# A gated linear recurrence and a two-layer block on one core: the last four groups of the block with seven products for eight, 64-column state products, and another written order

## The chip, the cores and the metric

The kernel runs on one core of one Trainium2 chip. A core has a matrix engine (PE), a vector engine (DVE), a scalar engine (ACT), GpSimd (POOL) and a queue for transfers (SP). The metric is the device time of one execution in microseconds (us), as the median of several runs. Each engine takes its instructions strictly in the order in which they were written for it; engines wait for each other through semaphores. SBUF is the working memory of 128 partitions; PSUM has eight banks of 2 KB in each partition, and only PE writes products there.

## The reference

```python
B, H, S, D = 4, 8, 768, 48          # batch, heads, tokens, head size
mag = sqrt(a_re**2 + a_im**2); scale = minimum(mag, 0.999) / (mag + 1e-6)
a = (a_re + 1j * a_im) * scale
for t in range(S):                   # for every batch and head
    S_re, S_im = a[t][:, None] * state  (+ outer(k[t], v[t]) on the real part)
    y[t] = q[t] @ S_re               # 48 values
x = y as (B * S, H * D) = (3072, 384)
h = x @ w_in                         # (384, 2048)
g = maximum(h, 0) + alpha * minimum(h, 0)
out = g @ w_out                      # (2048, 384), float32 throughout
```

## The kernel before

**Two halves in one stream.** The recurrence is cut into 24 units (4 batches of 6 chunks of 128 tokens, all 8 heads at once). A unit (`unit`, line 645) rotates keys and queries on DVE, meets them in six levels by small products (`meet`, L680, into the two PSUM banks of tag "lv"), transposes the keys (L789, bank "misc"), copies them to `T` on ACT (L791), forms the state's update from `T` and `V` (L799, `ps_kv`, banks "misc" and "lv"), and sums the unit's result in `ps_y` (two banks of tag "y"; L819 and L843). The result goes through `T` to a buffer in DRAM (`ysc`, L862). Ahead of the units, nine tasks `gates` work out the decays and phases on DVE, ACT and POOL and write them to DRAM (`decs`, `phs`); units read them back.

**The two-layer block.** `all_mlp` (L928) runs over groups of tokens, `sizes` (L642): two groups of one chunk, ten of two chunks, two of one chunk. For each of 16 slices f of 128 hidden values, `features` (L883) adds three products into one PSUM bank of tag "h" (L891; 128 by 128 weights against 256 tokens), ACT takes the negative part (L898) and DVE finishes `g` (L900) in `g_sb`, a ring of 36 places of 128 columns. `outputs` (L905) then adds 16 products of 384 columns for each chunk (L910, bank "o"), ACT copies the sum out (L920) and SP sends it (L923). `features` and `outputs` are called in turn, so that their products alternate on PE. The eight banks are lv 2, misc 1, y 2, h 2, o 1.

**What sets the order.** Every task (nine `gates`, loads, weights, 24 units, x loads, the block) is a generator that yields once for each step, and the string `ORDER` (L30) names the task whose next step is issued; each engine's program is the steps that fall to it, in that order. Letters A to I are the gates, P to Z and a to m the units, n the loads of x, o the block. The arguments of a yield (an engine, a planned duration, events, rings) are a planner's; in this file they do nothing. Where a tile's buffer is in use, the instruction that writes it next waits.

In the written order the last step of the last unit stands 131 letters before the end; 277,248 columns of the block's products stand ahead of it on PE and 17,664 behind it. (A column is one column of the moving operand of one product; a product of f32 shows as two MATMUL records, so L910 has 768 records for 384 products.)

## Time and profile before

| | |
|---|---|
| median of 3 runs | 837.81 us (835.79 to 839.57) |
| the profiled execution | 837.42 us; span from its first to its last instruction 835.7 us |
| mean granted clock of PE | 0.992 |
| busy PE / PEld / DVE / ACT / POOL | 701.3 / 533.9 / 637.5 / 432.4 / 282.6 us |
| busy DVE in L900, the block's only DVE work | 97.9 us |
| last record of a unit on PE | ends at about 796 us |

The page gives the busy time of each engine, the span in 40 slices of 20.9 us with busy shares in tenths, and the costliest groups of instructions, each with the mean duration of one and the idle time that came before them on their engine. A list of instructions in order of time gives start, duration, engine, line, operation and how many were merged. A table by stretches gives busy time and instructions of each engine in each stretch. PEld is the loading of weights, which runs beside PE.

### The profile page before, as it was taken

How to read it: one execution, taken by the hardware profiler on the slowest of the kernel's cores; microseconds unless marked ns; L12 is line 12 of the kernel's file. 1: busy time of each engine (PE TensorE's matmuls, PEld its weight loads, DVE VectorE, ACT ScalarE, POOL GpSimd, SP SyncE). 2: the span in 40 equal slices, each digit the busy share in tenths (PEclk: the TensorE clock that was granted, in tenths of full speed). 3: DMA queues.
4: the chain of work that ended last, by engine and by line, in shares of the span. 5: the costliest groups of instructions: out<-in, count | busy, mean ns of one | idle time of the engine just before them, and what ended most of it. 6: DMA issues, size and time to landing. Idle time of an engine off the chain costs nothing.

```text
span 835.7 us, 25314 instructions
## 1 busy us (share of the span) xinstructions
PE 701.3 (84%) x10784; PEld 533.9 (64%) x10784; DVE 637.5 (76%) x905; ACT 432.4 (52%) x893; POOL 282.6 (34%) x352
## 2 busy tenths in 40 slices
PE   0001317589999999999999999999999999999998
PEld 0001316467777777777777777776777777777776
DVE  5988979999999998989978989896649555542112
ACT  7787678377556644863675366624333333323221
POOL 5379399357306620661453127303220000000000
PEclk9999999699999999999999999999999999999999
DMA  7584975885688479538863966457446635401110
GB/s 221 169 239 133 307 226 135 234 222 147 176 234 199 114 217 250 140 84 245 227 158 83 275 176 162 145 158 186 100 98 176 159 95 125 103 24 36 42 29 10
DMA packets 186984, 130.82 MB, mean 157 GB/s; under 512 B 74744, under 2 KB 177272, under 8 KB 186488
## 3 DMA queue, kind: packets, MB, share of 16 engines
q1 hardware_dynamic: 186872, 129.20, 57.6%
q8 instruction: 85, 1.39, 0.7%
q14 instruction: 27, 0.22, 0.1%
HBM read 100.82 MB, written 35.71 MB: 163 GB/s over the span
## 4 chain that ended last, share of the span: by engine, by line
PE 63%; DVE 12%; POOL 7%; DMA 7%; ACT 6%; issue 3%; SPq 2%; DVEq 0%; ACTq 0%; POOLq 0%
PE ps_o L910 25%; PE ps_h L891 24%; PE ps_lv L680 4%; POOL gate L341 3%; PE ps_kv L799 3%; PE ps_y L819 3%; DMA T<-decs 2%; DVE KQ L718 2%; PE ps_y L843 2%; POOL run L343 2%; DVE gate L341 2%; DMA PP<-phs 1%; DMA phs<-gate 1%; DVE gate L429 1%; PE ps_kt L789 1%
## 5 line engine op out<-in xcount | busy, mean ns | idle before, releaser
L891 PE MATMUL ps_h<-xT,w_in_sb 128*128 128x256 f32 (+1 forms) x1344 | 297.4, 355 | 13.7 <-DMA xT<-ysc 13.5
L910 PE MATMUL ps_o<-w_out_sb,g_sb 128*128 128x384 f32 x768 | 295.0, 499 | 3.3 <-DVE g_sb L900 2.7
L891 PEld LDWEIGHTS ps_h<-xT,w_in_sb 128*128 128x128 f32 x1344 | 234.8, 193 | 85.5 <-DMA xT<-ysc 12.9
L898 ACT ACTIVATE g_sb<-ps_h 128x256 f32<-128x256 f32 (+1 forms) x224 | 79.0, 353 | 214.4 <-PE ps_h L891 213.3
L900 DVE SCALAR_TENSOR_TENSOR g_sb<-g_sb,al,ps_h 128x256 f32<-128x256 f32 (+1 forms) x224 | 97.9, 437 | 118.9 <-ACT g_sb L898 118.3
L910 PEld LDWEIGHTS ps_o<-w_out_sb,g_sb 128*128 128x128 f32 x768 | 136.0, 191 | 56.2 <-DVE g_sb L900 4.6
L718 DVE TENSOR_TENSOR KQ<-KQ,T 96x1024 f32<-96x1024 f32 x120 | 147.8, 1232 | 27.0 <-PE ps_lv L680 16.4
L341 POOL TENSOR_TENSOR gate<-gate 128x72 f32<-128x72 f32 (+1 forms) x56 | 42.5, 759 | 177.2 <-ACT gate L371 170.9
L680 PE MATMUL ps_lv<-WQ 96*32 96x32 f32 x2304 | 34.5, 202 | 76.4 <-DVE WQ L663 53.7
L680 PEld LDWEIGHTS ps_lv<-WQ 96*32 96x32 f32 x2304 | 26.2, 115 | 98.1 <-DVE WQ L663 53.7
L741 ACT COPY WQ<-KQ 96x1024 f32<-96x1024 f32 x48 | 50.0, 1041 | 23.7 <-DVE KQ L718 23.6
L341 DVE TENSOR_TENSOR gate<-gate 128x576 f32<-128x576 f32 (+3 forms) x70 | 46.8, 669 | 1.0
L341 POOL TENSOR_TENSOR gate<-run,runs 128x12 f32<-128x12 f32 x46 | 36.8, 800 | 31.2 <-ACT runs L371 28.1
L757 ACT COPY W<-KQ 96x512 f32<-96x512 f32 x48 | 30.8, 642 | 27.3 <-DVE KQ L718 23.2
L429 DVE TENSOR_TENSOR gate<-gate 128x1152 f32<-128x1152 f32 (+2 forms) x36 | 44.5, 1257 | 0.1
L518 POOL TENSOR_SCALAR top<-top 128x768 f32<-128x768 f32 x16 | 39.7, 2486 | 14.3 <-ACT top L510 14.2
L694 ACT ACTIVATE A<-ps_lv,columns 128x64 f32<-128x64 f32 x144 | 37.6, 335 | 8.4 <-PE ps_lv L680 8.3
L799 PEld LDWEIGHTS ps_kv<-V,T 64*96 64x96 f32 x704 | 35.9, 167 | 9.1 <-issue 4.6
L857 ACT COPY T<-ps_y 48x256 f32<-48x256 f32 x96 | 32.0, 365 | 18.2 <-PE ps_y L843 17.4
L321 POOL TENSOR_TENSOR gate<-gate 128x72 f32<-128x72 f32 (+5 forms) x24 | 22.5, 939 | 54.8 <-DVE gate L321 53.8
L799 PE MATMUL ps_kv<-V,T 64*96 64x48 f32 x704 | 38.9, 252 | 2.1 <-ACT T L791 2.0
L819 PE MATMUL ps_y<-A,VL 64*48 64x64 f32 x2304 | 38.8, 221 | 0.3 <-issue 0.3
(104 smaller groups left out, 943.7 us busy)
## 6 DMA issues: line engine op xcount, KB each, us to landing
T<-decs SPq DMA_DIRECT2D x48, 384.0 KB
PP<-phs SPq DMA_DIRECT2D x24, 387.0 KB
KQ<-in_q_dram SPq DMA_DIRECT2D x48, 192.0 KB
decs<-gate SPq DMA_DIRECT2D x7, 1152.0 KB
phs<-gate SPq DMA_DIRECT2D x14, 576.0 KB
KQ<-in_k_dram SPq DMA_DIRECT2D x40, 192.0 KB
vsc<-in_v_dram SPq DMA_DIRECT2D x48, 144.0 KB
VL<-vsc SPq DMA_DIRECT2D x48, 144.0 KB
```

Source lines behind the costliest of these rows:

```text
L341: on(4 * k).tensor_tensor(out=m, in0=w[:, 1::-1].unsqueeze(2).to_broadcast([P, 2, 2, k]), in1=pairs_of(u), op=ALU.mult)
L429: TT(out=m[:, a], in0=U5[:, 1 + a], in1=turned(off3, o)[:, a].unsqueeze(1).unsqueeze(3).to_broadcast([P, L // 2, nb, 2]), op=ALU.mult)
L518: nc.gpsimd.tensor_scalar(out=top, in0=top, scalar1=F64_SMALL, scalar2=None, op0=ALU.max)
L680: nc.tensor.matmul(t[64 * i + j:64 * i + j + HC // 2, p], lhsT=keys(n, g), rhs=queries(n, g), start=True, stop=True)
L718: nc.vector.tensor_tensor(out=x, in0=x if x0 is None else x0, in1=m, op=ALU.mult)
L741: nc.scalar.copy(z.rearrange("p i n t -> p i (n t)").rearrange("p i (m h) -> p m i h", h=h), bass.AP(tensor=KQ.tensor, offset=KQ.offset + ...
L799: nc.tensor.matmul(kv[s][:, n], lhsT=T[rows, n, 0:D2], rhs=V[rows, n // 2, (n % 2) * D:(n % 2 + 1) * D], start=True, stop=True)
L819: nc.tensor.matmul(o, lhsT=Vp[h][64 * i:64 * i + 64, s, e_ * D:(e_ + 1) * D], rhs=a, start=False, stop=False)
L891: nc.tensor.matmul(p, lhsT=w_in_sb[:, f // 2, kk, f % 2 * P:(f % 2 + 1) * P], rhs=x_of[m][:, kk], start=(kk == 0), stop=(kk == NK - 1))
L898: nc.scalar.activation(gt, p, AF.Relu, scale=-1.0)
L900: nc.vector.scalar_tensor_tensor(out=gt, in0=gt, scalar=al_1[:, f:f + 1], in1=p, op0=ALU.mult, op1=ALU.add)
L910: nc.tensor.matmul(sums[0], lhsT=gt[:, c * P:(c + 1) * P], rhs=w_out_sb[:, f], start=(f == 0), stop=(f == NF - 1))
```

## The change

1. **Groups.** `sizes` becomes two groups of one chunk and eleven of two; the last four (`LATE` = 9 and up, eight of the 24 chunks) take other functions.
2. **First part of the late groups** (`late_features`): two slices f and two chunks are done at once. Of the three parts of the contraction, one stays as it was (two products of 256 columns); the other two form, with the two slices and the two chunks, a 2 by 2 by 2 scheme of blocks, done with seven products of 128 columns in Winograd's form of Strassen's scheme. So nine products with 1408 columns stand for six with 1536. Sums of weights (`mixes`) and of x (`tx`) are formed ahead on DVE; the sums of products are formed by five DVE instructions out of two PSUM banks, "y" and "h" in turn. ACT takes the negative parts from SBUF, and DVE finishes `g`.
3. **Second part** (`late_outputs`, a task of its own, letter q): two slices f, two chunks and two halves of the 384 output columns, with seven products of 192 columns for four of 384 (1344 columns for 1536). POOL forms the four sums of `g` (128 by 128 each). The seven products are kept apart over all eight pairs of slices, in the four banks lv, lv, misc and o, and are put together at the end of a group by one ACT and seven DVE instructions. As the units use lv and misc too, these products come after the last unit.
4. **State products** (L799): two products of 64 columns of weights each in place of one of 96, with a second, smaller copy ahead of them on ACT that fills `T` up to 128 columns.
5. **Order.** `ORDER` is another. In it 203,776 columns of the block's products stand ahead of the last unit's last step and 80,896 behind it. All eight steps of `mixes`, and the first part of group 9 up to its fourth pair, stand ahead of it. `ysc` gets eight DRAM buffers in place of four.

The tasks `mixes` (p) and `late_outputs` (q) are added to the plan behind the block.

```diff
@@ ORDER = (
...
@@ -639,7 +643,8 @@
...
-    sizes = [1, 1] + [MC] * ((NU - 4) // MC) + [1, 1]
+    sizes = [1, 1] + [MC] * ((NU - 2) // MC)
+    LATE = len(sizes) - 4
...
@@ -787,17 +792,19 @@
             t = ps.tile([P, HP, D2], F32, tag="misc", name="ps_kt")
             for p in range(4):
                 nc.tensor.transpose(t[:, p], KQ[:, 1, 4 * i + p], ident[:D2, :D2])
-            e = yield ACT(HP * D2, e, ("decays", u))
+            e = yield ACT(HP * P + 80, e, ("decays", u))
             nc.scalar.copy(T[:, 4 * i:4 * (i + 1), 0:D2], t)
+            nc.scalar.copy(T[:, 4 * i:4 * (i + 1), D2:P], t[:, :, 0:P - D2])
             R["misc"].put(e)
-        e = yield PE(0.72, e, ("V", u), *[("state", u - 1)] * (u > 0), takes=(R["misc"],) if last else (R["misc"], R["lv"]), mode=2, n=8 if last else 16)
+        e = yield PE(0.72, e, ("V", u), *[("state", u - 1)] * (u > 0), takes=(R["misc"],) if last else (R["misc"], R["lv"]), mode=2, n=16 if last else 32)
         V = L["V"]
-        kv = [ps.tile([P, H, D], F32, tag=tag, name="ps_kv", bufs=n)[0:D2] for tag, n in (("misc", 1), ("lv", 2))[:2 - last]]
+        kv = [ps.tile([P, H, D], F32, tag=tag, name="ps_kv", bufs=n) for tag, n in (("misc", 1), ("lv", 2))[:2 - last]]
         for n in range(H):
-            for s in range(1 if last else 2):
-                rows = slice(HC * s, HC * (s + 1))
-                nc.tensor.matmul(kv[s][:, n], lhsT=T[rows, n, 0:D2],
-                                 rhs=V[rows, n // 2, (n % 2) * D:(n % 2 + 1) * D], start=True, stop=True)
+            for j in range(0, P, HC):
+                for s in range(1 if last else 2):
+                    rows = slice(HC * s, HC * (s + 1))
+                    nc.tensor.matmul(kv[s][j:j + HC, n], lhsT=T[rows, n, j:j + HC],
+                                     rhs=V[rows, n // 2, (n % 2) * D:(n % 2 + 1) * D], start=True, stop=True)
         ek = e
         for s in range(2):
             for part in range(2):
@@ -828,7 +835,7 @@
             nc.vector.tensor_tensor(out=St, in0=before, in1=T[0:D2, :, TL - 4 + s:TL - 3 + s].to_broadcast([D2, H, D]),
                                     op=ALU.mult)
...
-            nc.vector.tensor_tensor(out=St, in0=St, in1=kv[s], op=ALU.add)
+            nc.vector.tensor_tensor(out=St, in0=St, in1=kv[s][0:D2], op=ALU.add)
...
-            ysc_of[g] = dram.tile([H * D, sizes[g] * P], F32, tag="ysc", name="ysc")
+            ysc_of[g] = dram.tile([H * D, sizes[g] * P], F32, tag="ysc", name="ysc", bufs=8)
...
-        made, jobs = {}, [(m, c, f) for m, n in enumerate(sizes) for c in range(n) for f in range(NF)]
+        made, jobs = {}, [(m, c, f) for m, n in enumerate(sizes[:LATE]) for c in range(n) for f in range(NF)]
         for m in range(len(sizes)):
             for f in range(NF):
-                new = yield from features(m, f)
+                new = (yield from features(m, f)) if m < LATE else (yield from late_features(m, f // 2)) if f % 2 else None
                 for _ in range(2):
-                    if jobs[0][0::2] not in made:
+                    if not jobs or jobs[0][0::2] not in made:
                         break
                     j = jobs.pop(0)
                     yield from outputs(*j, *made[j[0::2]])
                     if j[2] == NF - 1:
                         break
                 made[m, f] = new
-        for j in jobs:
-            yield from outputs(*j, *made[j[0::2]])
+    g_of = {}
+    mixed = [None]
+    HM = DM // 2
+    W2 = w_out_sb.rearrange("p (j two) (s e) -> p j two s e", two=2, s=2)
+    def mixes():
+        for j in range(0, NF // 2, 2):
+            t = yield DVE(4 * 2 * HM, ("gates", len(GATES) - 2), *[("w_out", 2 * i) for i in (j, j + 1)])
+            if j == 0:
+                mixed[0] = work.tile([P, 6 * NK * GT], F32, tag="gate", name="mix", bufs=2)
+            M = mixed[0][:, 0:4 * NF // 2 * HM].rearrange("p (j k e) -> p j k e", k=4, e=HM)[:, j:j + 2]
+            w = W2[:, j:j + 2]
+            for o, a, b_, op in ((M[:, :, 0], w[:, :, 0, 1], w[:, :, 0, 0], ALU.subtract),
+                                 (M[:, :, 2], w[:, :, 1, 1], w[:, :, 0, 1], ALU.subtract),
+                                 (M[:, :, 1], M[:, :, 2], w[:, :, 0, 0], ALU.add),
+                                 (M[:, :, 3], M[:, :, 1], w[:, :, 1, 0], ALU.subtract)):
+                nc.vector.tensor_tensor(out=o, in0=a, in1=b_, op=op)
+            done["mixes", 0, j] = done["mixes", 0, j + 1] = t
+        for j in range(0, NF // 2, 2):
...
+    tx = {}
+    def late_features(m, j):
+        TT = nc.vector.tensor_tensor
+        if j == 0:
+            done["tx", m] = yield DVE(4 * P, ("x", m), takes=(R["WQ"],))
+            x = x_of[m].rearrange("p k (c t) -> p k c t", c=2)
+            slot = spare.pop(0)
+            tx[m] = slot, work.tile([P, 4, P], F32, tag=f"WQ{slot}", name="tx", bufs=1)
+            t1, t2, t3, t4 = [tx[m][1][:, i] for i in range(4)]
+            for o, a, b_ in ((t1, x[:, 0, 1], x[:, 0, 0]), (t3, x[:, 1, 1], x[:, 0, 1]),
+                             (t2, x[:, 1, 1], t1), (t4, x[:, 1, 0], t2)):
+                TT(out=o, in0=a, in1=b_, op=ALU.subtract)
+        for at in range(9):
+            e = yield PE(0.22, ("tx", m), ("mixes", 1, j), takes=((R["h"], R["h"]) if j % 2 else (R["y"],)) if at == 0 else ())
+            if at == 0:
+                x = x_of[m].rearrange("p k (c t) -> p k c t", c=2)
+                t1, t2, t3, t4 = [tx[m][1][:, i] for i in range(4)]
+                w = w_in_sb[:, j].rearrange("p k (two e) -> p k two e", two=2)
+                M = mixed[1][:, 0:4 * NF // 2 * P].rearrange("p (j k e) -> p j k e", k=4, e=P)[:, j]
+                s1, s2, s3, s4 = [M[:, i] for i in range(4)]
+                both = x_of[m][:, 2]
+                terms = ((0, slice(0, 2), w[:, 2, 0], both), (0, 3, w[:, 0, 0], x[:, 0, 0]), (0, 0, w[:, 1, 0], x[:, 1, 0]),
+                         (0, 2, s2, t2), (0, 1, s4, x[:, 1, 1]),
+                         (1, slice(0, 2), w[:, 2, 1], both), (1, 3, s3, t3), (1, 2, s1, t1), (1, 0, w[:, 1, 1], t4))
+                if j % 2:
+                    X = [ps.tile([P, 4, P], F32, tag="h", name="ps_h", bufs=2) for _ in range(2)]
+                else:
+                    y_ = ps.tile([P, 2, 512], F32, tag="y", name="ps_y")
+                    X = [y_[:, i].rearrange("p (k t) -> p k t", k=4) for i in range(2)]
+            k, place_, lhs, rhs = terms[at]
+            o = X[k][:, place_]
+            if place_ == slice(0, 2):
+                o = o.rearrange("p k t -> p (k t)")
+            nc.tensor.matmul(o, lhsT=lhs, rhs=rhs, start=(at in (0, 5)), stop=(at in (4, 8)))
+            if at == 4:
+                ea = e
+        if j == NF // 2 - 1:
+            R["xT"].put(e)
+            R["WQ"].put(e)
+            spare.append(tx[m][0])
+        f = 2 * j
+        i, ring, _ = place(m, f)
+        assert i % 4 == 0 and place(m, f + 1)[0] == i + 2
+        r = yield ACT(P, ea, takes=(R["St"],))
+        t0 = work.tile([P, P], F32, tag="St", name="t0", bufs=3)
+        nc.scalar.copy(t0, X[0][:, 3])
+        G = g_sb.rearrange("p r (f s) -> p (r f) s", f=12)[:, i:i + 4]
...
+        r = yield DVE(2 * P, r, takes=(ring, ring))
+        TT(out=pair(G, 0, 3), in0=pair(X[0], 0, 2), in1=twice(t0), op=ALU.add)
+        R["St"].put(r)
+        r = yield DVE(2 * P, e)
+        TT(out=pair(G, 1, 2), in0=pair(X[1], 2, 3), in1=twice(G[:, 3]), op=ALU.add)
+        r = yield DVE(2 * P)
+        TT(out=pair(G, 3, 2), in0=pair(X[1], 2, 0), in1=twice(G[:, 2]), op=ALU.add)
+        r = yield DVE(P)
+        TT(out=G[:, 1], in0=X[0][:, 1], in1=G[:, 1], op=ALU.add)
+        r1 = yield DVE(P)
+        TT(out=G[:, 3], in0=X[1][:, 1], in1=G[:, 3], op=ALU.add)
+        for _ in range(2 if j % 2 else 1):
+            R["h" if j % 2 else "y"].put(r1)
+        a1 = yield ACT(2 * P, r, takes=(R[1],))
+        rl = work.tile([P, 4, P], F32, tag="A1", name="rl", bufs=2)
+        nc.scalar.activation(rl[:, 0:2], G[:, 0:2], AF.Relu, scale=-1.0)
+        a2 = yield ACT(2 * P, r1)
+        nc.scalar.activation(rl[:, 2:4], G[:, 2:4], AF.Relu, scale=-1.0)
+        for h in range(2):
+            r = yield DVE(2 * P + 45, (a1, a2)[h])
+            g2 = G[:, 2 * h:2 * h + 2].rearrange("p f s -> p (f s)")
+            nc.vector.scalar_tensor_tensor(out=g2, in0=rl[:, 2 * h:2 * h + 2].rearrange("p f s -> p (f s)"),
+                                           scalar=al_1[:, f + h:f + h + 1], in1=g2, op0=ALU.mult, op1=ALU.add)
+            done["g", m, f + h] = r
+            g_of[m, f + h] = g2
+        R[1].put(r)
+    def late_outputs():
...
+        for m in range(LATE, len(sizes)):
+            for j in range(NF // 2):
+                x = yield POOL(4 * P, ("g", m, 2 * j), ("g", m, 2 * j + 1), takes=() if j % 4 else (R["KQ"],))
+                if j % 4 == 0:
+                    S_ = work.tile([P, 4, 4, P], F32, tag="KQ", name="sums", bufs=3)
+                (a11, a21), (a12, a22) = [[g_of[m, f][:, c * P:(c + 1) * P] for c in range(2)] for f in (2 * j, 2 * j + 1)]
+                s1, s2, s3, s4 = [S_[:, j % 4, i] for i in range(4)]
+                for o, a, b_, op in ((s1, a21, a22, ALU.add), (s3, a11, a21, ALU.subtract),
+                                     (s2, s1, a11, ALU.subtract), (s4, a12, s2, ALU.subtract)):
+                    nc.gpsimd.tensor_tensor(out=o, in0=a, in1=b_, op=op)
+                w = W2[:, j]
+                for at in range(7):
+                    e = yield PE(0.33, x, ("mixes", 0, j), takes=() if j or at else (R["lv"], R["lv"], R["misc"], R["o"]))
+                    if not (j or at):
+                        banks = [ps.tile([P, 2, HM], F32, tag=tag, name="ps_m", bufs=n)
+                                 for tag, n in (("lv", 2), ("lv", 2), ("misc", 1), ("o", 1))]
+                    if at == 0:
+                        M = mixed[0][:, 0:4 * NF // 2 * HM].rearrange("p (j k e) -> p j k e", k=4, e=HM)[:, j]
+                        terms = ((0, 0, a11, w[:, 0, 0]), (1, 0, a12, w[:, 1, 0]), (0, 1, s2, M[:, 1]), (1, 1, s3, M[:, 2]),
+                                 (2, 0, a22, M[:, 3]), (2, 1, s1, M[:, 0]), (3, 0, s4, w[:, 1, 1]))
+                    k, half, lhs, rhs = terms[at]
+                    nc.tensor.matmul(banks[k][:, half], lhsT=lhs, rhs=rhs, start=(j == 0 and half == 0), stop=(j == NF // 2 - 1 and at in (2, 3, 5, 6)))
+                    if at == 4:
+                        for f in (2 * j, 2 * j + 1):
+                            place(m, f)[1].put(e)
+                if j % 4 == 3:
+                    R["KQ"].put(e)
+            p1, p6, p2, p7, p4, p5, p3 = [banks[i // 2][:, i % 2] for i in range(7)]
+            tmp = mixed[0][:, 4 * NF // 2 * HM:4 * (NF // 2 + 1) * HM].rearrange("p (k e) -> p k e", k=4)
+            row = sum(sizes[:m]) * P
+            ot = tops[0].rearrange("p (c s e) -> p c s e", c=2, s=2)
+            t = yield ACT(HM, e)
+            nc.scalar.activation(tmp[:, 0], p1, AF.Copy, scale=scale)
+            for at, (o, p_, by, add) in enumerate(((ot[:, 0, 0], p2, scale, tmp[:, 0]), (tmp[:, 1], p6, scale, tmp[:, 0]),
+                                                   (tmp[:, 2], p7, scale, tmp[:, 1]), (ot[:, 1, 0], p4, -scale, tmp[:, 2]),
+                                                   (ot[:, 1, 1], p5, scale, tmp[:, 2]), (tmp[:, 3], p5, scale, tmp[:, 1]),
+                                                   (ot[:, 0, 1], p3, scale, tmp[:, 3]))):
+                t = yield DVE(HM + 60, t, takes=(R["ot"],) if at in (0, 3) else ())
+                STT(out=o, in0=p_, scalar=by, in1=add, op0=ALU.mult, op1=ALU.add)
+                if at in (1, 2):
+                    R["lv"].put(t)
+                if at == 4:
+                    t2 = t
+                if at == 5:
+                    R["misc"].put(t)
+            R["o"].put(t)
+            for c, t in ((1, t2), (0, t)):
+                t = yield DMA(197, t)
+                nc.sync.dma_start(out[row + c * P:row + (c + 1) * P], ot[:, c].rearrange("p s e -> p (s e)"))
+                R["ot"].put(t)
...
         plan.add(all_mlp())
+        plan.add(mixes())
+        plan.add(late_outputs())
...
```

## The prediction

> **What bounds the kernel now.** I read the slices of the page first, then a table of six stretches, then the groups of PE and DVE, last single instructions in order of time.
>
> ```profile
> PE   0001317589999999999999999999999999999998
> DVE  5988979999999998989978989896649555542112
> POOL 5379399357306620661453127303220000000000
> ```
> ```profile
> 0.00:140.00 140.00, 27.08 (x660) 22.15 (x660) 116.64 (x192) 103.99 (x155) 95.67 (x111) 1.00 0.74 213
> 140.00:200.00 60.00, 46.02 (x993) 36.34 (x993) 58.19 (x83) 37.94 (x76) 33.30 (x36) 0.89 0.75 200
> 200.00:560.00 360.00, 356.90 (x5725) 271.22 (x5726) 328.97 (x431) 202.64 (x432) 136.38 (x173) 1.00 0.67 177
> 560.00:680.00 120.00, 119.22 (x1783) 89.57 (x1782) 76.65 (x104) 45.03 (x114) 17.25 (x34) 1.00 0.54 137
> 680.00:796.00 116.00, 116.00 (x1431) 87.84 (x1429) 49.02 (x76) 34.27 (x89) 0.00 (x0) 1.00 0.28 70
> ```
> The columns are the stretch, its length, then busy time (and count) of PE, PEld, DVE, ACT, POOL, then PE's clock. From 200 us on PE has no idle time worth the name: 592 of 596 us up to 796. Before that it loses 127 of 200 us, because units and x aren't there yet. DVE is nearly full too, 97% from 140 to 200 and 91.4% (328.97/360) from 200 to 560, and then falls to 42% by the last units. So the end is set by PE's work, and DVE has slack only late. The last unit leaves PE at 796 us; 17,664 columns of the block follow it.
>
> ```profile
> L910 PE MATMUL ps_o<-w_out_sb,g_sb 128*128 128x384 f32 x768 | 295.0, 499 | 3.3 <-DVE g_sb L900 2.7
> L900 DVE SCALAR_TENSOR_TENSOR g_sb<-g_sb,al,ps_h 128x256 f32<-128x256 f32 (+1 forms) x224 | 97.9, 437 | 118.9 <-ACT g_sb L898 118.3
> ```
> A mean of 499 ns is no price, as products overlap; I take prices from starts:
> ```profile
> 760.87 1.45 PE L910 MATMUL ps_o<-w_out_sb,g_sb 128*128 128x384 f32 x4
> 763.45 1.45 PE L910 MATMUL ps_o<-w_out_sb,g_sb 128*128 128x384 f32 x4
> ...
> 828.41 0.83 PE L891 MATMUL ps_h<-xT,w_in_sb 128*128 128x128 f32 x6
> 829.73 0.83 PE L891 MATMUL ps_h<-xT,w_in_sb 128*128 128x128 f32 x6
> ```
> From 760.87 to 763.45, two products of 384 and three of 256 columns pass: 1536 columns in 2.58 us, 1.68 ns each. From 828.41 to 829.73, three of 128 and one of 384: 768 columns in 1.32 us, 1.72 ns. So products of 128 columns, with a weight load for each, cost 2% more per column. I take 1.70.
>
> **The products saved.** A pair of slices of a late group goes from 3072 to 1408 + 1344 = 2752 columns; 8 pairs in 4 groups save 32 x 320 = 10,240 columns, at 1.68 ns 17.2 us; 2% on the 88,064 columns left in smaller products gives 1.8 back (bounds 0 and 3.5). **15.4 us** less of PE's 701.
>
> **State products.** These lines are one unit:
> ```profile
> 641.15 1.56 PE L799 MATMUL ps_kv<-V,T 64*96 64x48 f32 x32
> 642.64 0.30 PE L810 MATMUL ps_y<-ident,nothing 64*48 64x256 bf16 x4
> 642.76 1.51 PE L819 MATMUL ps_y<-A,VL 64*48 64x64 f32 x96
> 644.21 0.46 PE L680 MATMUL ps_lv<-WQ 96*32 96x32 f32 x32
> ```
> L799 holds PE 1.49 us for 32 records, 47 ns each, although each streams only 48 columns. L819, with weights of 64 rows by 48, passes 96 records in 1.45 us, 15 ns each; 64 columns alone would take 54 ns (64 x 1.68 / 2 records), so three to four run at a time. The new form is 64 records of 64 by 64 weights, the shape of L819's quarters: 64 x 15 = 0.96 us. Bounds: 64 x 24 = 1.5 (nothing gained) and 0.72 (by 48 columns instead of 64). At 0.96 a unit saves 0.53, 24 units **12.7 us** (bounds 0 and 18). The Trainium skill has a rule against this part, in TensorE: Matmul & The Clock Gate, section "Wait — 56ns, not 53.3ns?": starts of products never come closer than about 25 ns. By that rule 64 records would take an estimated 1.6 us and the part would cost 0.1 us a unit. The rows disagree, 15 ns in L819 and 8 in L680 (32 in 0.27 us). The added ACT copies (48 at about 0.28 us, L898's price for 128 columns) go to an engine 52% busy; one per unit lies ahead of L799, which waits 2.0 us for ACT in the whole run. I charge nothing; uncovered it is 24 x 0.28 = 7 us.
>
> **The move.** This decides. The late second parts need the banks lv and misc, so they stand behind the last unit: 80,896 columns instead of 17,664. At 1.70 ns that is 137.5 us of PE after the last unit, so the time is the last unit's end, **T**, plus 137.5 plus a tail. The tail: before, ACT's 0.49 us and a transfer lie behind the last product, which ends at about 832.3 (span 835.7). Now ACT copies 192 columns (0.33, between L898's 0.28 at 128 and 0.38 at 256), then seven dependent DVE instructions of 192 columns (0.41, between L900's 0.34 at 128 and 0.47 at 256), 2.9 us, then the same transfer, 2.9: **6.1 us**.
>
> T from PE: ahead of it stand 203,776 columns, at 1.69 ns 344 us. A unit's own work is (701.3 - 495.5) / 24 = 8.6 us, where 495.5 is all 294,912 columns at 1.68; 24 units less 12.7 make 193. With the 127 us lost at the start and 1% of waits, T = 344 + 193 + 127 + 5 = 669.
>
> T from DVE: all its work but L900 is 637.5 - 97.9 = 539.6 us and stays. To it come L900 of groups 0 to 8 (32 at 0.34, 112 at 0.47: 64), four pairs of group 9 (each three instructions of 256 at 0.47, two of 128 at 0.34, two of 256 at 0.47: 3.0, so 12), four differences of x (1.2) and `mixes`: 16 of 384 columns at 0.60 (L828's 0.586, L341's 0.633) and 16 of 256 at 0.43 (L343's 0.359 to 0.455), 16.5 us. Sum 633, and none of it is hidden on DVE. The start stays as it is, 116.6 busy by 140 and 58.2 more by 200, so 458 us are left from 200 on. At L900's surroundings of now (91.4%) T = 701; at 97% 672; at 100% 658. In the stretch from 200 to 560, 31 us were idle, of which 10.5 in front of L900 and 7.2 in front of L718, both for late products. With PE full, DVE's idle time cost nothing then; now it does, and fewer products of the block stand ahead of each unit. I take 95.5%: **T = 200 + 458/0.955 = 680**, span 680 + 137.5 + 6.1 = 823.6. With the 1.7 us that lie around the span (837.42 - 835.7) that is **825**; the median of the runs shown, 837.81, is 0.4 us off the profiled execution, which I leave out.
>
> **What stays hidden behind T.** A late pair needs 4.7 us of PE (2752 columns) and 3.0 of DVE. From the last product of its first part to its second part: two DVE instructions of 256, two of 128, ACT 0.38, DVE 0.47, together 2.5 us, then four on POOL. The written order leaves 5.5 to 10 us of other products between (17.6 for the first pair). The nearest row of POOL:
> ```profile
> L402 POOL TENSOR_TENSOR gate<-gate x16: 368/621/4214, 73.4 to 613.3; 128x126 f32<-128x126 f32 x14, 128x84 f32<-128x84 f32 x2
> ```
> Shortest 0.37 us, median 0.62, longest 4.2: four take 1.5 to 2.5, so the chain is 4.0 to 5.0 us, inside 5.5. Between groups the banks come free 0.33 + 2.9 = 3.2 us after the last product; the order leaves 3.9 to 4.8 us of first parts there. Uncovered, three such gaps cost up to 10 us. SP issues one x load fewer and as many output transfers; eight `ysc` buffers take nobody's time.
>
> **Rivals.** (1) **DVE holds the last unit back**: density stays at 91.4%, T = 701, time 701 + 143.6 + 1.7 = 846, slower. It decides from T = 697, 92.2%. For it: that is the density measured over 360 us. Against: that idle time was free, and 140 to 200 shows 97%. (2) **Both engines pack**: T = 669, time 814. For it: PE had 99% from 200 to 560. Against: DVE would need 97.7%. (3) **POOL's sums come late.** At L402's mean of 1.15 us four take 4.6 and the chain 7.1, beyond most of the 5.5 to 7 us distances of groups 11 and 12 and some of group 10. With some 20 pairs short by 1 us and half of that paid (two pairs are always under way), 10 us: 835, no change. For it: POOL's waits beside a busy DVE, 4.2 us at worst. Against: DVE is only two thirds busy there, and most of its operands come from PSUM. The Trainium skill (GPSIMD Engine Reference, section "Engine selection") advises VectorE for two-input elementwise work, as about twice as fast; L402's 0.37 at best beside 0.34 for DVE doesn't show the factor. (4) The seven products save nothing because weight loads bind: 15 us more, 840. The 1.72 ns row speaks against it.
>
> **How the numbers follow.** Likeliest as above 0.43 (815 to 833 by T between 670 and 688), rival 1 0.22, rival 2 0.18, rival 3 0.13, rival 4 0.04. A difference of 0.5% (4.2 us) is what a measurement can tell from none. Faster: 0.40 of the likeliest, rival 2's 0.18, 0.04 of rival 3: 0.62. Slower: 0.19 of rival 1, 0.02 each of rivals 3 and 4: 0.23. Same: 0.15. Range 811 to 845: PE's bound with more of the state products saved, and T at 700.
>
> **What would show it.** The last unit leaves PE near 680 (696 or later: rival 1), with DVE at 95% from 200 on. PE stays at 9 in all slices behind it. L799 holds PE about 1 us a unit. If PE waits there for the POOL sums by more than 5 us in all, rival 3. I am wrong if the time is over 845 or PE idles before T by more than 25 us beyond the start.

## The result and the profile after

| | before | changed |
|---|---|---|
| median, first comparison | 837.96 us (835.79 to 839.57) | 869.12 us (861.88 to 881.27) |
| ratio | 1 | 1.0345 (1.0257 to 1.0433) |
| median, run again (`e1_same`) | 840.42 us | 872.38 us (871.05 to 874.24), 1.0364 (1.0326 to 1.0402) |
| last product of the last unit starts, **T** | 795.9 us | 723.8 us |
| end of the span | 835.7 us | 869.3 us |
| from T to the end | 39.8 us | 145.5 us |

The forecast was 825 us, T at 680 and 143.6 us behind it. The kernel is slower by 3.6%. Each ratio is to the kernel before, run beside it, with a 95% interval. The profile taken first fell in a disturbed run, the slowest (881.27 us), which the ratio leaves out, so the lines below are from the profile of the second comparison (871.05 us); every "changed kernel" below is that one. T is read from one profiled execution of each kernel, and executions of one kernel lie some us apart, so differences of a few us in T are not read.

The page of the changed kernel, slices of 21.7 us in tenths:
```profile
PE   0001407969999999898899789989999999999997
DVE  5988969999989899799899697878977973656564
POOL 5477589266118204731632281450000021343433
```
Between slices 17 and 27 PE has 7s and 8s among its 9s, where before it had 9s alone; behind T (from slice 34 on) it is full. The table by stretches says how much that is (stretch, length, busy time and count of PE, PEld, DVE, ACT, POOL, PE's clock, share of the DMA engines, GB/s), first the kernel before, then the changed one:
```profile
200.00:560.00 360.00, 356.90 (x5725) 271.22 (x5726) 328.97 (x431) 202.64 (x432) 136.38 (x173) 1.00 0.67 177
560.00:796.00 236.00, 235.22 (x3212) 177.41 (x3210) 125.67 (x179) 79.29 (x203) 17.25 (x34) 1.00 0.41 104
```
```profile
200.00:560.00 360.00, 330.41 (x6018) 244.82 (x6007) 324.17 (x427) 202.59 (x446) 138.97 (x175) 0.98 0.69 178
560.00:724.00 164.00, 155.53 (x3088) 115.71 (x3086) 132.42 (x197) 67.38 (x180) 24.14 (x47) 0.98 0.56 133
```
From 200 us to T PE lost 3.9 us before and 38.1 us now, and its clock is 2% lower. DVE does 456.6 us of work in that time, almost exactly the 458 of the forecast, but it needs 524 us for it: 87.1%. And behind T:
```profile
726.00:866.00 140.00, 138.93 (x942) 135.78 (x940) 82.35 (x235) 28.33 (x88) 49.47 (x112) 1.00 0.07 20
```
PE is busy for 138.9 of 140 us. So the second half of the working held, and nearly the whole loss lies ahead of T: 43.8 of the 45.7 us by which the span (869.3) misses the forecast's 823.6. PE's waits between 200 us and T (engine, line, what it waited for: total us, times, longest), before and changed:
```profile
PE ps_lv L680 <- ACT W L757: 1.5, 4, 0.6
PE ps_kv L799 <- ACT T L791: 0.5, 1, 0.5
```
```profile
PE ps_lv L685 <- ACT W L762: 17.5, 11, 4.5
PE ps_kv L806 <- ACT T L797: 5.1, 4, 3.8
PE ps_y L826 <- issue: 4.5, 4, 2.6
PE ps_kt L794 <- ACT T L797: 4.0, 2, 3.2
```
PE now stands in front of the units' own products until ACT has copied their operands. Since PE takes its program in order, the block's products behind them stand as well. The four rows make up 31.1 of the 38.1 us.

### The profile page after: what moved, and what is told of

It reads as the page before. It is cut to its first block, busy times and chain, and to the rows that moved or that the text cites. A ratio compares the mean times of both kernels' runs of the same rounds, so it can differ in the third digit from the quotient of the medians.

```text
span 879.5 us, 27856 instructions
## 1 busy us (share of the span) xinstructions
PE 703.8 (80%) x11776; PEld 558.6 (64%) x11776; DVE 711.6 (81%) x1125; ACT 442.3 (50%) x953; POOL 339.5 (39%) x480
## 4 chain that ended last, share of the span: by engine, by line
PE 47%; DVE 19%; POOL 12%; ACT 8%; DMA 6%; issue 5%; SPq 3%; DVEq 0%; ACTq 0%; POOLq 0%
PE ps_o L917 11%; PE ps_h L898 10%; PE ps_m L1092 8%; POOL gate L345 5%; DVE KQ L723 5%; PE ps_y L1017 4%; PE ps_h L1017 4%; PE ps_y L826 3%; POOL gate L347 3%; PE ps_lv L685 3%; DMA T<-decs 2%; DVE gate L345 2%; POOL run L347 2%; DVE gate L433 2%; PE ps_kv L806 2%
## 5 line engine op out<-in xcount | busy, mean ns | idle before, releaser
L898 PE MATMUL ps_h<-xT,w_in_sb 128*128 128x256 f32 (+1 forms) x864 | 207.3, 371 | 19.4 <-DVE w_in_sb L526 19.0
L917 PE MATMUL ps_o<-w_out_sb,g_sb 128*128 128x384 f32 x512 | 206.4, 519 | 3.3 <-DVE g_sb L907 2.5
L898 PEld LDWEIGHTS ps_h<-xT,w_in_sb 128*128 128x128 f32 x864 | 155.1, 197 | 64.9 <-DMA xT<-ysc 20.1
L1080 POOL TENSOR_TENSOR sums<-g_sb 128x128 f32<-128x128 f32 x64 | 28.7, 470 | 228.8 <-DVE g_sb L1061 228.8
L917 PEld LDWEIGHTS ps_o<-w_out_sb,g_sb 128*128 128x128 f32 x512 | 91.6, 196 | 39.9 <-DVE g_sb L907 3.8
L905 ACT ACTIVATE g_sb<-ps_h 128x256 f32<-128x256 f32 (+1 forms) x144 | 51.9, 360 | 83.5 <-PE ps_h L898 82.5
L907 DVE SCALAR_TENSOR_TENSOR g_sb<-g_sb,al,ps_h 128x256 f32<-128x256 f32 (+1 forms) x144 | 63.6, 442 | 28.5 <-ACT g_sb L905 28.2
L826 PE MATMUL ps_y<-A,VL 64*48 64x64 f32 x2304 | 48.6, 236 | 17.5 <-issue 13.1
L826 PEld LDWEIGHTS ps_y<-A,VL 64*48 64x48 f32 x2304 | 44.3, 134 | 22.4 <-issue 17.2
L685 PE MATMUL ps_lv<-KQ,W 96*32 96x32 f32 x1536 | 25.2, 208 | 30.6 <-ACT W L762 30.0
L1092 PE MATMUL ps_m<-mix,sums 128*128 128x192 f32 x192 | 43.4, 326 | 0.0
```

The source lines that it names most:

```text
L685: nc.tensor.matmul(t[64 * i + j:64 * i + j + HC // 2, p], lhsT=keys(n, g), rhs=queries(n, g), start=True, stop=True)
L826: nc.tensor.matmul(o, lhsT=Vp[h][64 * i:64 * i + 64, s, e_ * D:(e_ + 1) * D], rhs=a, start=False, stop=False)
L898: nc.tensor.matmul(p, lhsT=w_in_sb[:, f // 2, kk, f % 2 * P:(f % 2 + 1) * P], rhs=x_of[m][:, kk], start=(kk == 0), stop=(kk == NK - 1))
L905: nc.scalar.activation(gt, p, AF.Relu, scale=-1.0)
L907: nc.vector.scalar_tensor_tensor(out=gt, in0=gt, scalar=al_1[:, f:f + 1], in1=p, op0=ALU.mult, op1=ALU.add)
L917: nc.tensor.matmul(sums[0], lhsT=gt[:, c * P:(c + 1) * P], rhs=w_out_sb[:, f], start=(f == 0), stop=(f == NF - 1))
```

## The experiments

**Who sets T: PE's work, DVE's work, or the state products?** Four runs: the changed kernel again, the same with its new state products taken back, the kernel before with them alone, and the changed kernel with PE lightened ahead of T.

`e1_same`, no edit. 

> The changed kernel itself once more, for a profile that is not of its slowest run (881 us) and for the spread. Both theories: 862 to 873 us; behind the last unit some 145 us as in the first profile (734 to 879.5). Theory A (instructions): PE's idle time for no shown reason ('issue') in the sums of a unit's result is again over 10 us in all and in other units than before. Theory B (mutual waits): that idle time is under 5 us in the faster profile, and DVE is still 85 to 90% busy between 200 us and the last unit's end.

Measured: 872.38 us, 1.0364 (1.0326 to 1.0402). The result stands. Idle time for no shown reason in front of the sums (L826) is 4.5 us and DVE is 87.1% busy from 200 us to T, as theory B had it.

`e2_kv96`, the state products and the copy as before:
```diff
-            nc.scalar.copy(T[:, 4 * i:4 * (i + 1), D2:P], t[:, :, 0:P - D2])
...
-            for j in range(0, P, HC):
...
+                nc.tensor.matmul(kv[s][:, n], lhsT=T[rows, n, 0:D2],
```


> The changed kernel with the state products of 96 columns again and without the second copy on ACT; the order is unchanged. Theory A: the doubled burst of small products outruns the loading of PE's instructions; with it gone the idle time for no shown reason is under 2 us, the clock stays full, and the last unit ends 20 us earlier: about 845 us, with less spread. Theory B (engines wait for each other in the new order, the burst is a minor matter): the stalls go too, but PE has 0.5 us more per unit, 12 in all: 862 to 875 us, same as the changed kernel.

Measured: 870.08 us, 1.0341 (1.0288 to 1.0394), no different from `e1_same`, as theory B had it. In the changed kernel the new state products are worth nothing.

`e3_before_kv64`, the reverse: the kernel before with the products of 64 columns and the copy (part 4 of the change, as its diff has it). 

> The kernel before with the state products of 64 columns and the second copy on ACT alone; its own order. Prediction's term: 12.7 us less of PE, which sets the end: 825 us. Theory A: stalls for no shown reason appear here too and eat the gain: 833 to 842 us. Theory B: the gain of the term, 824 to 828 us, as PE is full and has nothing to wait for.

Measured: 865.77 us, 1.0283 (1.0233 to 1.0332). Both expectations fell: alone, this part costs the kernel before about 25 us, more than either theory allowed. Its groups on PE (busy us, mean ns | idle before, what ended it), the kernel before first:
```profile
L799 PE MATMUL ps_kv<-V,T 64*96 64x48 f32 x704 | 38.9, 252 | 2.1 <-ACT T L791 2.0
L819 PE MATMUL ps_y<-A,VL 64*48 64x64 f32 x2304 | 38.8, 221 | 0.3 <-issue 0.3
```
```profile
L801 PE MATMUL ps_kv<-V,T 64*64 64x48 f32 x1408 | 29.6, 226 | 2.7 <-ACT T L792 2.6
L821 PE MATMUL ps_y<-A,VL 64*48 64x64 f32 x2304 | 44.9, 226 | 20.4 <-issue 20.1 <-DMA VL<-vsc 0.2
```
L801 itself is 9.3 us shorter, as meant. But the unit sums right behind it, whose code did not change, take 6.1 us more and stand idle for 20.1 us with nothing that the profile shows to wait for ("issue"). One of these gaps, in order of time:
```profile
666.32 1.51 PE L821 MATMUL ps_y<-A,VL 64*48 64x64 f32 x94
670.90 0.27 PE L821 MATMUL ps_y<-A,VL 64*48 64x64 f32 x2 [3.06 <-issue]
```
94 of 96 records run (a product of f32 shows as two), then 3.06 us of nothing, then the last two.

`e4_less_pe`, the changed kernel with the last of three contraction steps of the first layer left out in groups 2 to 8 (48 us of PE):
```diff
+            if m < 2 or kk < NK - 1:
```


> The changed kernel without one of the three parts of the contraction in the first layer of groups 2 to 8 (112 products of 256 columns less, 48 us of PE, all ahead of the last unit's end; nothing else changes). If PE's work sets the last unit's end: 48 us less, about 818 us. If DVE's work or the engines' mutual waits set it: 850 to 866 us, that is at most 15 us less, with PE idle in its place.

Measured: 871.08 us, 1.0357 (1.0309 to 1.0405); T 728.6. PE's work alone does not set T: idle time took its place, 70.5 us between 200 us and T where there were 38.1.

**What is it in the state products?** `e5_copy`, the kernel before with ACT's second copy alone:
```diff
+            nc.scalar.copy(T[:, 4 * i:4 * (i + 1), D2:P], t[:, :, 0:P - D2])
```


> The kernel before with the second copy on ACT alone; state products of 96 columns as they were. It tells the two halves of the state part apart. If the burst of 64-column products is what made the part cost 25 us: 837 to 842 us, PE's idle time for no shown reason stays under 1 us. If the copy is (ACT's queue, or the chain ahead of the products): 855 us or more.

Measured: 839.07 us, 0.9976 (0.9943 to 1.0008): the copy is free. The 25 us come with the products, not with the copy.

`e6_spaced`, `e3_before_kv64` with some 1536 columns of the block's products written between the state products and the unit sums, in 21 of 24 units; only letters of `ORDER` change places. 

> The kernel before with 64-column state products, and the order changed in one way: for 21 of 24 units some 1536 columns of the two-layer block (2.6 us of PE) are drawn in between the state products and the sums of the unit's result, so that the two bursts of small products no longer follow each other. Theory A (PE's instructions don't arrive as fast as a burst of small products uses them up): most of the 25 us of idle time for no shown reason is gone, and with it the half clock behind it; 826 to 834 us. If the products themselves cost the time, or the idle time has another cause: 860 us or more, as without the spacing.

Measured: 866.89 us, 1.0296 (1.0230 to 1.0362). "Issue" in front of the sums fell from 20.1 to 4.9 us, but the unit's result came later and PE waited 28.7 us for ACT's W (19.5 in `e3_before_kv64`): no gain. Of the two expectations the second was met (860 us or more), though the gaps did shrink. So the gaps in front of the sums are not shown to be the whole of the 25 us.

`e11_before_half_y` and `e12_kv64_half_y`: both leave out the three upper levels of the unit sums, 48 of 96 records; the first with the state products of before, the second with the new ones.
```diff
-                for h in LEVELS[3 * part:3 * part + 3]:
+                for h in () if part else LEVELS[0:3]:
```


> Control: the kernel before with the three upper levels of the unit sums (48 of the 96 records behind each state burst) left out. Less TensorE work of some 24 x 48 x 15 ns = 17 us: 815 to 838 us.

> The same with state products of 64 columns and the copy. If it is the number of small products in a row that TensorE cannot be supplied with (64 + 4 + 48 here against 32 + 4 + 96 before, which ran without such gaps), the gaps are gone and this takes 8 to 13 us less than the control. If it is the state products themselves, whatever follows them, it takes some 25 us more than the control.

Measured: 828.78 us, 0.9895 (0.9855 to 0.9935), and 832.36 us, 0.9934 (0.9913 to 0.9956). Neither expectation was met in full: with half the sums behind them the new products cost 3.6 us (the intervals overlap), not 25, but they did not gain 8 to 13 either. The idle time of the sums in `e12_kv64_half_y`:
```profile
L821 PE MATMUL ps_y<-A,VL 64*48 64x64 f32 x1152 | 23.1, 221 | 5.7 <-issue 5.7
```
So most of the stall needs both, 64 records of state products and 96 of sums in a row: it goes with the number of small products in one stretch. That PE's instructions do not arrive fast enough is a guess; no row names a cause.

**Does DVE set T?** `e7_mix2`, every instruction of `mixes` twice (16.5 us more DVE work), and `e8_no_stt`, the changed kernel without DVE's L907 in groups 2 to 8 (53 us less), in this order:
```diff
+                for _ in range(2):
                     nc.vector.tensor_tensor(out=o, in0=a, in1=b_, op=op)
...
+        if m < 2:
             nc.vector.scalar_tensor_tensor(out=gt, in0=gt, scalar=al_1[:, f:f + 1], in1=p,
```


> The changed kernel with each of the 32 sums of weights done twice: 16.5 us more work on DVE, all ahead of the last unit's end. If DVE's work sets that end, 16 us more: about 888 us. If mutual waits set it and DVE has gaps to take this in: at most 5 us more, 872 to 877.

> The changed kernel without DVE's last step of g in groups 2 to 8 (ACT's negative part is passed on as it is): 112 instructions, 53 us of DVE less, and with them the waits of DVE for ACT there (20 to 28 us); PE's work is unchanged. If DVE's work and its waits for the block's products set the last unit's end: 40 us earlier or more, under 832 us. If PE's, or the loads and the gates on POOL: 855 us or more.

Measured: 882.01 us, 1.0457 (1.0390 to 1.0524), and 873.88 us, 1.0355 (1.0291 to 1.0419) with T at 725.5. Against `e1_same` the doubled work costs 0.0093 of 840, some 8 of its 16.5 us, between the two expectations and with intervals that overlap a little; T moved by 12 us in the profiles (723.8 to 736), all of it behind the seventeenth unit. The 53 us taken out of DVE give nothing back. So one busy share of DVE does not describe T, though work put in among the last units is not free. A run without the sums of weights ahead of T was not made, so what the 16.5 us of `mixes` in the changed kernel cost stays open.

**Does the block set T at all?** `e9_no_block` keeps of groups 2 to 8 one of three contraction steps, every fourth product row of the second layer, and no L907 (121,856 columns, at 1.69 ns about 206 us of PE, and 53 us of DVE gone). `e10_short_gates` leaves out the serial products of the decays on POOL behind the first.
```diff
+            if m < 2 or kk == 0:
...
+        if m < 2 or f % 4 == 0:
```
```diff
-            t = yield from product(run[:, :, :, j + 1], ends[:, :, :, j], run[:, :, :, j], f, NK, t)
+            t = yield from product(run[:, :, :, j + 1], ends[:, :, :, j], run[:, :, :, j], f, NK, t, g > 0 and j > 0)
```


> The changed kernel with groups 2 to 8 keeping only the first of the two contraction steps of their first layer, every fourth row of their second layer, and no third operation of a row's activation (about 230 us of TensorE's and 53 us of VectorE's work left out, all of it ahead of the last unit). Theory that the units' own chain (loads, gates on POOL, the order on ACT) sets the last unit's time: it stays at 700 us or later and the run takes 845 us or more. Rival, that a unit waits for the group's block on whichever engine: the last unit comes by 650 us and the run takes under 795 us.

> The changed kernel with the serial products of the decays on POOL left out after the first step, for every gate but the first (so the decays that the units use are others; about ten small POOL operations fewer for each gate). If POOL's chain of the gates sets the pace of the units up to 580 us (27 us a unit), units come 2 us or more apart faster and the last at 700 us or before: 845 us or less. If it does not: the last unit at 720 to 730 us, 866 to 876 us.

Measured: 850.24 us, 1.0147 (1.0088 to 1.0205), T 699.6; and 865.13 us, 1.0316 (1.0271 to 1.0360), T 713.9. The short gates land between the two expectations: T is 10 us earlier, but the profiled execution (861.24 us) was the fastest of its four, and the interval overlaps that of `e1_same`. With the larger part of the block gone, the last unit comes only 24 us earlier, at the edge of what the theory of the units' own chain allowed (700 us or later). PE's waits in `e9_no_block` between 200 and 700 us:
```profile
PE ps_lv L685 <- ACT W L762: 55.1, 24, 5.7
PE ps_lv L685 <- ACT WQ L746: 13.9, 13, 2.1
PE ps_lv L685 <- DVE KQ L723: 13.0, 15, 1.8
PE ps_kv L806 <- ACT T L797: 10.8, 12, 2.7
```
The work that was taken out has turned into the same waits as in the changed kernel, the first of them three times as long. They are the steps of a unit: DVE turns keys, ACT copies them, PE meets them. But this run does not show the units at full speed. With PE idle so much, its clock fell:
```profile
200.00:560.00 360.00, 254.98 (x5772) 184.00 (x5774) 310.52 (x361) 207.64 (x475) 152.13 (x206) 0.75 0.72 189
```
The units' own products took longer for it: over the last seven units the busy times of their six lines on PE add up to 54.1 us in the changed kernel and 70.5 us here, 2.3 us more a unit.

**The loads of the decays.** `e14_no_decs` leaves these loads out from the third unit on (the units use what lies in two fixed tiles); `e15_no_decs_no_block` does that and `e9_no_block`'s cuts.
```diff
+                if u < 2:
                     nc.sync.dma_start(T[rows], scr.rearrange("(h d) c s -> d h c s", d=D)[:, :, at])
```


> The changed kernel with the loads of the decays (768 KB a unit) left out from the third unit on; the units use what is in the two buffers. If waiting for these loads sets the pace (they stand for 8 to 10% of the chain of waits between 380 and 480 us), the last unit comes 25 us or more sooner, by 700 us: 847 us or less. If the pace is set by DVE with the gates beside the units, it comes at 715 to 728 us and the run takes 860 to 876 us.

> The changed kernel without the decay loads from the third unit on and, as in the earlier run without most of the block's work, groups 2 to 8 cut down. That run alone brought the last unit from 723 to 699 us. If the loads are what held it there, it now comes by 675 us: 825 us or less. If what is left is the units' own chain over DVE, ACT and PE and the gates, it stays at 688 to 699 us: 838 to 850 us.

Measured: 863.30 us, 1.0283 (1.0246 to 1.0320), T 715.3; and 831.34 us, 0.9898 (0.9866 to 0.9930), T 685.3. The loads are worth 8.5 us of T by themselves, the edge of what was expected if they are not the cause, and 14 us once the block is gone, between the two expectations: a part, not the cause.

`e13_y_out` and `e16_before_y_out` take the unit's result out of the decays' tile and let ACT issue its transfer, in the changed kernel and in the kernel before:
```diff
-                    yT = T[:, 0:4, 0:P].rearrange("p (i s) t -> p i s t", i=2)
+                    yT = L["KQP"][:, 0, 0:4].rearrange("p (i s) t -> p i s t", i=2)
...
-            nc.sync.dma_start(ysc[e_, :, :, cg * P:(cg + 1) * P],
+            nc.scalar.dma_start(ysc[e_, :, :, cg * P:(cg + 1) * P],
```


> The changed kernel with a unit's result taken out of the tile of the decays (it goes into the unit's own tile of keys and queries, which is dead by then), and its two transfers issued by ACT instead of SP; all results stay as they were. Now a decay load waits for the result transfer of the unit two before (both its buffer and SP's order), which takes 2 to 4.4 us, and then takes 5 to 7 us itself. If that loop sets the units' pace, each unit comes 0.5 us or more sooner, the last at 715 us or before: 862 us or less. If not: 868 to 876 us.

> The kernel before with the same result path (own tile, ACT issues). TensorE is full from 200 us on and the last unit's time does not set its end, so both theories expect no change within 0.5%: 834 to 842 us.

Measured: 932.38 us, 1.1113 (1.1066 to 1.1159), and 876.99 us, 1.0448 (1.0407 to 1.0489). Both expectations fell. SP's waits, changed kernel and `e13_y_out`:
```profile
SPq L598 <- DMA ysc<-T: 20.5, 20, 2.4
```
```profile
SPq L631 <- DMA ysc<-KQ: 93.1, 17, 11.1
SPq L584 <- DMA ysc<-KQ: 22.0, 3, 17.4
```
Loads of keys (L584) and of v (L631), early in SP's written order, now wait for a result that comes late, and every load queued behind them waits as well: 115 us of waits on the results' transfers for 20.5. Why a load of v waits for it isn't shown, and ACT now also spends 18.0 us on issuing the 48 transfers, so the two edits are not told apart. What the runs show is that loads that come late hold the units back, and that in the kernel before, whose end I had put down to PE's work, units 37 us later (T 833.2) made the end 37.6 us later (873.3).

**Two groups moved in place of four.** `e17_late_two` and `e18_late_two_b` give only the last two groups the seven products, keep the state products of before, and use an order of their own.
```diff
-    LATE = len(sizes) - 4
+    LATE = len(sizes) - 2
```


> A version built on the reading that the last unit cannot come much before 700 to 725 us but may well come at 755: only the last two groups have the seven-product form, state products as before (96 columns), units in the order of the kernel before, drawn closer together from gate's end on. 252,928 columns stand ahead of the last unit and 36,864 behind it. If TensorE stays full up to there, the last unit comes 24,320 columns x 1.69 ns = 41 us earlier than before, at 755 us, and the end follows 62.7 us of products, the 6 us by which the kernel before lies over that sum, and a tail of 6 us later: 830 us of span against 835.7, so 829 to 835 us and a ratio of 0.990 to 0.998. If drawing the last units closer already opens gaps in TensorE, 838 us or more.

> The same idea with the order mended: in the run before, the ACT and DVE steps of the block had slipped behind the unit steps that stood next to them, and the units lagged 17 us by the sixteenth. Here the written order is that of the kernel before, step for step, up to the seventeenth unit, and only the last seven are drawn together. 245,760 columns ahead of the last unit, 44,032 behind. If TensorE stays full, the last unit comes at 743 us and the run takes 829 to 835 us (ratio 0.990 to 0.998). If units drawn to 22 us apart open gaps in TensorE as in the changed kernel (5% of 175 us), 836 to 845 us. If it is 855 us or more as in the run before, the place of the ACT and DVE steps was not what cost it.

Measured: 862.44 us, 1.0262 (1.0233 to 1.0291), T 790.2; and 866.86 us, 1.0331 (1.0301 to 1.0361), T 772.0. In the first the ACT and DVE steps of the block had moved against the units' and the seventeenth unit was 17 us late. The second follows the kernel before exactly up to there:
```profile
200.00:560.00 360.00, 357.00 (x5729) 271.93 (x5728) 329.95 (x433) 202.56 (x432) 129.85 (x172) 1.00 0.67 177
560.00:772.00 212.00, 192.22 (x2967) 142.71 (x2965) 129.49 (x188) 69.68 (x175) 18.91 (x34) 0.94 0.45 111
```
Up to 560 us it is the kernel before. Then, where 53 us of block products were taken from among the last seven units, PE stands idle for 19.8 us of 212 at a clock of 0.94, and T comes 24 us earlier in place of 53. It is the same kind of loss behind an unchanged first part, though the sums of weights stand among these units too. By what was expected of it, a time over 855 us says that the place of the block's ACT and DVE steps was not what cost the run before. A better written order, for two groups or for four, may exist; none was found.

## Why the prediction was wrong, step by step

**The end from T: right.** Predicted 137.5 us of products and a tail of 6.1, together 143.6; measured 145.5. Two small misses partly cancel in it: the products behind the last unit's last one (82,432 columns, 1536 more than counted) took 141.2 us, and the tail 4.4, as ACT's copy and the first DVE steps of the end were done before the last product was. It held in every variant that kept the four late groups and their order behind T: 145.6 in `e10_short_gates`, 145.6 in `e14_no_decs`, 147.2 in `e9_no_block`. The price was 1.71 ns a column against 1.70 forecast. Rival 4, no saving at all, would need 1.88 (98,304 columns at 1.68 spread over 88,064), and PE has no wait behind T, so rivals 3 and 4 are out. POOL's sums took 469 ns in the mean of this half of them, between the bounds of 0.37 and 0.62:
```profile
L1080 POOL TENSOR_TENSOR sums<-g_sb 128x128 f32<-128x128 f32 x64 | 28.8, 469 | 219.4 <-DVE g_sb L1061 219.4
```
**T: the step that failed.** The forecast took T = 200 + 458/0.955 = 680, with "I take 95.5%". The work was right to 1.4 us; the share of DVE's time that it fills was 87.1%, below the 91.4% that I had used as the worst case. The reasoning behind it was that DVE's idle time "cost nothing then; now it does", so that it would shrink. It did not shrink: 12.9% of the time from 200 us to T, where the kernel before had 8.6% from 200 to 560. Nor does T follow either engine's work: taking 53 us from DVE (T 725.5), or 48 us from PE (T 728.6), did not bring T forward, as waits took the place of the work. What I had treated as two engines to be filled behaves as a chain of dependent steps, DVE to ACT to PE and back, with loads and the gates beside it.

The pace shows it (T by units, from the starts of the last products of each unit on PE):

| | unit 2 | unit 17 | unit 24 | us per unit, 2 to 17 | 17 to 24 |
|---|---|---|---|---|---|
| before | 149 | 568 | 795 | 27.9 | 32.4 |
| changed | 155 | 562 | 723 | 27.1 | 23.0 |
| gates cut, `e10_short_gates` | 154 | 552 | 713 | 26.5 | 23.0 |
| block cut, `e9_no_block` | 155 | 542 | 699 | 25.8 | 22.4 |
| block and loads cut, `e15_no_decs_no_block` | 155 | 536 | 685 | 25.4 | 21.3 |

My 680 asked for 16.9 us a unit from the seventeenth on ((680 - 562) / 7). Without most of the block and without the loads the chip made 21.3. The lower clock of these runs is in that figure; if all of its 2.3 us a unit lay on the chain, an estimate for full clock is 19.0, still above 16.9. The kernel before ran units 2 to 17 at 27.9 us each with 99% of PE filled in between; I read that as PE's bound. But the changed kernel without most of the block still needed 25.8, so the block's products had mostly filled waits that were there anyway; for the kernel before itself this is argued, as no run took its block out. By my bound by PE, T was to come 127 us earlier (796 to 669); it came 72 earlier.

**Rivals.** The time by rival 1 (T 701, 846 us) was nearest, and had the right place, the stretch ahead of T; but its mechanism, DVE's work, is not what the runs show, as T stayed with 53 us of that work gone. Rival 2 is out by 55 us of T: PE stood idle for 38.1 us in place of 5 from 200 us on, its own work there took 485.9 us where 344 and 193, less the 70 done by 200 us, make 467, and 3 us more were lost at the start. Both conditions by which I said I would be wrong were met: over 845 us, and PE idle for 34 us more ahead of T than before (38.1 against 3.9).

**State products: a term mis-sized.** Predicted 12.7 us saved (bounds 0 and 18). The group itself fell from 38.9 to 30.4 us, 8.5, and one block takes 1.08 us where 0.96 was forecast, 17 ns a record. (The sum also counted 24 full blocks; the 704 records of L799 are 22 blocks of 32.)
```profile
458.82 1.15 PE L806 MATMUL ps_kv<-V,T 64*64 64x48 f32 x64
459.90 0.70 PE L898 MATMUL ps_h<-xT,w_in_sb 128*128 128x256 f32 x2
```
The floor of about 25 ns between starts that the Trainium skill gives (TensorE: Matmul & The Clock Gate, section "Wait — 56ns, not 53.3ns?") does not hold for these records. The sums behind the block give part of the gain back, the changed kernel first and then `e2_kv96`, the same with the state products of before:
```profile
L826 PE MATMUL ps_y<-A,VL 64*48 64x64 f32 x2304 | 45.6, 229 | 7.6 <-issue 4.5
L824 PE MATMUL ps_y<-A,VL 64*48 64x64 f32 x2304 | 43.2, 229 | 3.0 <-DMA VL<-vsc 2.2
```
PE was waiting for the units anyway, and what the products saved it stood idle: 38.1 us between 200 us and T against 27.4 in `e2_kv96`. So the term is worth nothing in the changed kernel, and where PE is full the part loses 25 us (`e3_before_kv64`). The bounds looked at the block alone and left out what stands right behind it. Charging nothing for ACT's copy was right (`e5_copy`).

**What stays open.** How the chain's pace divides. The block gave 24 us of T, with a lower clock against it, the loads 8.5 to 14, the gates at most 10; they don't add up to a single cause. The rest, DVE's own unit and gate work (311.95 of 360 us in `e15_no_decs_no_block` from 200 to 560) with its round trips over ACT and PE, wasn't taken apart. Nor is it shown how much of the pace comes from the written order of the steps, which all variants of the changed kernel share.

## What to carry to other kernels

A full engine need not be what sets the pace: before moving work away from between dependent steps, ask how fast those steps come without it, and check the forecast against the shortest spacing that the trace shows, not against a busy share alone. In the kernel before no two units from the second on come closer than 22.4 us; seven such steps from unit 17 at 562 us give an estimated T of 719, near the 723.8 that came. (It is no strict floor: single units of the changed kernel came 17 us apart.) A share of 91% on one engine is no measure of what 458 us of its work will take in another arrangement. Many tiny products in a row should be priced together with what follows them.

## What the runs showed of the hardware

- **PE gaps without a releaser.** In the kernel before, stretches of 64 + 4 + 96 small records in a row drew 20.1 us of "issue" gaps (eleven, up to 3.8 us), 32 + 4 + 96 drew 0.3, and 64 + 4 + 48 drew 5.7, each in front of records of the sums. In the changed kernel, where PE waits for the units as well, 64 + 4 + 96 drew 4.5 and 32 + 4 + 96 (`e2_kv96`) 0.8.
- **The clock pays for idleness.** With PE 71% busy from 200 to 560 us (`e9_no_block`, 254.98 of 360) the granted clock there was 0.75; at 86% (`e4_less_pe`) it was 0.95, at 92% 0.98, at 99% 1.00. Products that are left run slower: the transposes of keys (L794) took 325 ns in the mean in `e9_no_block` and 264 in the changed kernel. That gives back part of what was taken out, and makes a run with work taken out a poor measure of the rest at full clock.
- **Loads early in SP's queue** that wait for a late result go with 60 us more (`e13_y_out`), without any added transfer; the same run also moved the results' transfers to ACT.
